# A gated mix of linear attention and a feed-forward layer: where early low parts are stored, where the key-value bursts stand, and where the fold of wq is done

## The chip, the cores and the metric

The kernel runs on one core of one Trainium2 chip. The metric is the device time of one execution in microseconds (us): the kernel before took 517.11 us in the median of three runs. The engines are named as the profile names them: PE is TensorE (PEld its weight loads), DVE is VectorE, ACT is ScalarE, POOL is GpSimd, and SP is SyncE, which here only issues transfers (DMAs).

## The reference

The input `x` has 2048 rows of 512. The output is `g * a + (1 - g) * b`, where the gate `g` is a sigmoid of one dot product per row.

```
a: qkv = x @ wqkv;  pq, pk = q, k times w_phi per head (32 heads of 16)
   phi = concat(softmax(p), softmax(-p))          for q and for k
   kv  = sum over rows of phi_k (x) v;  z = sum of phi_k
   o   = (phi_q kv) / (phi_q z + 1e-6);  a = o @ wo
b: h = relu(x @ w1 + b1) ** 2  (512 -> 1792);  b = h @ w2 + b2
out = g * a + (1 - g) * b
```

All of it is float32.

## The kernel before

**Products in three parts.** Every large operand is split into a high part (rounded to the type `fp32r`) and a low part (the remainder). ACT casts the high part, DVE subtracts to get the low part (`split`, L65 and L68). `mm3` (L73 to L75) then makes three matmuls: high by high, low by high, high by low. A tile of 128x512 has 256 KB.

**Two sweeps over the rows.** The 1792 hidden units are 14 chunks of 128, 7 to a sweep. Each sweep goes over four blocks of 512 rows. A work item `t` is one chunk in one block: `up` makes the hidden chunk `u` (12 matmuls, then relu and square on ACT and a split), and `down` adds it to the block's four output tiles `d0` to `d3` (12 matmuls). `up` runs two items ahead of `down` (`LAG`). In the first sweep the keys and values are made beside this work, in the second the queries and the attention's output.

**FFN weights.** The first sweep uses chunks 0 to 6 in each of its four blocks. In block 0 each weight is fetched (`fetch`) into one of four staging tiles `in` and split (`ready_later`). Its low part is also stored in DRAM by `keep` (tile `lkept`). In blocks 1 to 3, `again` fetches the weight and loads the stored low part, and `again_ready` only casts the high part on ACT. The high and low tiles of w1 and of w2 come from rings of three buffers (`fpool`, `NSTR`), so the fourth tile must wait until the first was used, and, where it is stored, until its store has landed. The very first product of w1 chunk 0 is done in plain float32 and needs no low part.

**Keys and values.** For each of eight pairs `p` of row tiles, seven products (`p1` to `p7`) make k (already multiplied by w_phi) and v, by a scheme that saves one of eight block products. Three accumulators take turns in two PSUM banks: `kx` and `kz` share one bank, `ky` has the other. `features` reads `kx` four times on DVE (maximum, minimum and two subtractions, L347 to L350), ACT takes the exponential, and DVE sums, inverts and multiplies (L355, L357, L361). So `kz` can't begin before those four reads are done. `do_kv` is the key-value burst: 64 products of 32x32 into one PSUM tile `kvps` of the ring that `u` uses.

**The fold.** `fold("q")` multiplies wq by w_phi: 64 small matmuls (`foldq`) that fill both buffers of the `u` ring and both PSUM banks of the keys and values. Four DVE transposes (L222, `wqin`) empty these.

**What sets the order.** `at(slot, f, ...)` puts a step into a table that the main loop reads, two slots to a work item. A scheduling layer below the kernel then places each instruction in its engine's queue by its own estimate of when operands are ready. `tc.high_priority` moves instructions ahead, and `tc.issue_after` forces one behind another. Each engine runs its queue strictly in order, so an instruction that waits holds all behind it. SP's queue is one of these: at most eight transfers are under way, since each waits for the landing of the eighth before it.

Of the kernel before, what the change touches and what calls it, by code (L numbers as in the profile page):

```python
# [18 lines left out]
NK = D // P  # L19
SB = 512  # L20
NB = S // SB
NC = SB // P
NF = F // P
NFH = NF // 2
LAG = 2
# [3 lines left out]
NPAIR = S // P // 2  # L29
NSTR = 3  # L30
AHEAD = 150
SUMS = ("t1", "t2", "t15", "k2")


@with_exitstack
def tile_gated_mix(ctx: ExitStack, tc: tile.TileContext, xT, xn, wqT, wkT, wphi, wv, wo, w1, b1, w2, b2, gw, out):
    nc = tc.nc
# [14 lines left out]
    st, up_w, down_w = {}, {}, {}  # L52
# [47 lines left out]
    raw = {}  # L100
# [29 lines left out]
    def ready_later(nm, fc, *elo):  # L130
        with tc.issue_after(st["act"].ins):
            ready(nm, fc, *elo)
# [67 lines left out]
    def fold(nm):  # L200
        wph, t = st["wphi"], st["wT", nm]
        pss = [ps_u.tile([P, 512], F32, tag="u", name=f"fold{nm}{r}") for r in range(2)]
        pss += [p.tile([P, 512], F32, tag="s", name=f"fold{nm}") for p in banks]

        def mm(g, r, q):
            rows, cols = slice(32 * r, 32 * r + 32), slice(g * P + 32 * r, g * P + 32 * r + 32)
            return nc.tensor.matmul(pss[r][32 * q:32 * q + 32, g * P:(g + 1) * P], wph[rows, cols],
                                    t[g][rows, :].rearrange("r (k q i) -> r k q i", q=4, i=32)[:, :, q, :],
                                    start=True, stop=True, skip_group_check=True)


        todo = [(g, r, q) for g in range(NK) for q in range(4) for r in range(4)]
        with ExitStack() as stack:
            for i, x in enumerate(todo):
                st["up"] = mm(*x)
                if i < 4:
                    stack.enter_context(tc.issue_after(st["up"].ins))
        w = work.tile([P, 2, 4, NG, 32], F32, tag="phiT", name=f"w{nm}in", bufs=1).rearrange(
            "p u r g s -> p (u r g s)").rearrange("p (k g r s) -> p k g r s", k=NK, g=NK, r=4)
        for r in range(4):  # L220
            with tc.high_priority(offset=AHEAD):
                nc.vector.transpose(w[:, :, :, r, :].rearrange("p k g s -> p g k s"),  # L222
                                    pss[r].rearrange("p (g k i) -> p g k i", g=NK, i=32))
        st["w", nm] = [w[:, k].rearrange("p g r s -> p (g r s)") for k in range(NK)]

    def foldq_load():
# [105 lines left out]
    def project(c, xs, ws, nm):  # L332
        ps = bank(nm)
        sc = slice(c * P, (c + 1) * P)
        for k in range(NK):
            mm3(ps, xs[k], ws[k], sc, ALL, k == 0, k == NK - 1)
        return ps

    def exps(ps, tag="e"):

        pv = ps.rearrange("p (h f) -> p h f", f=DH)
        mx = small.tile([P, H], F32, tag="mx", name="mx")
        mn = small.tile([P, H], F32, tag="mn", name="mn")
        e = work.tile([P, H, 2, DH], F32, tag=tag, name="e", bufs=2 if tag == "e" else 1)
        bc = lambda t: t.unsqueeze(2).to_broadcast([P, H, DH])
        with tc.high_priority(offset=AHEAD):
            nc.vector.tensor_reduce(mx, pv, AX.X, ALU.max)  # L347
            nc.vector.tensor_reduce(mn, pv, AX.X, ALU.min)
            nc.vector.tensor_tensor(e[:, :, 0, :], pv, bc(mx), ALU.subtract)
            nc.vector.tensor_tensor(e[:, :, 1, :], bc(mn), pv, ALU.subtract)  # L350
        ef = e.rearrange("p h t f -> p (h t f)")
        nc.scalar.activation(ef, ef, AF.Exp)  # L352
        e3 = e.rearrange("p h t f -> p (h t) f")
        sm = small.tile([P, 2 * H], F32, tag="sm", name="sm")
        nc.vector.tensor_reduce(sm, e3, AX.X, ALU.add)  # L355
        r = small.tile([P, 2 * H], F32, tag="r", name="r")
        nc.vector.reciprocal(r, sm)  # L357
        return e3, r
# [114 lines left out]
    def down(t, c, dps):  # L473
        sw, b, i = work_list[t]
        end = i == NFH - 1 or t == last - 2 and c == NC - 1
        st["down"] = mm3(dps[c], hid[t], down_w[sw * NFH + i], slice(c * P, (c + 1) * P), ALL, i == 0, end)
# [13 lines left out]
    def start():  # L490
        w = work.tile([P, 2, 4, NG, 32], F32, tag="phiT", name="win", bufs=1).rearrange("p u r g s -> p (u r g s)")
        t = st["xr", 0] = [work.tile([P, 2 * D], F32, tag="tb", name="xin", bufs=2) for _ in range(2)]
        raw["w1", 0] = w[:, :D]
        xs = [t[k // 2][:, k % 2 * D:(k % 2 + 1) * D] for k in range(NK)]
        for k in range(NK):
            nc.sync.dma_start(xs[k], xT[0, :, k, :])
        nc.scalar.dma_start(w[:, :D], w1[0])
        fetch("w1", 1, w[:, D:2 * D])
        fetch("w1", 2, w[:, 2 * D:3 * D])
        fetch("w2", 0, w[:, 3 * D:])  # L500
        fetch("w1", 3)
        fetch("w2", 1)
        t = [wpool.tile([P, 512], F32, tag=tag, name="fold") for tag in ("T40h", "T30h", "T30l", "T31h", "T31l")]
        st["wphi"] = t[0]
        nc.sync.dma_start(t[0], wphi)
        load_fold("k", wkT, t[1:])
        fetch("w1", 4)
        fetch("w2", 2)
        ps = ps_u.tile([P, SB], F32, tag="u", name="u")
        st["x", 0] = []  # L510
        for k in range(NK):
            kk = slice(k * P, (k + 1) * P)
            with tc.issue_after(st["up"].ins):
                st["up"] = nc.tensor.matmul(ps, raw["w1", 0][:, kk], xs[k], start=k == 0, stop=k == NK - 1)
            hi, lo = x_tiles(0, k)
            split(xs[k], hi, lo, nc.scalar, nc.vector)
            st["x", 0].append((hi, lo))

        t = raw.pop(("w1", 1))
        hi, lo = up_w[1] = ffn_tiles("w1", 1)  # L520
        for j in (slice(0, P), slice(P, 512)):
            nc.scalar.activation(hi[:, j], t[:, j], AF.Copy)
        nc.vector.tensor_tensor(lo, t, hi.bitcast(F32), ALU.subtract)
        i = ready("w1", 2)
        with tc.issue_after(i.ins):
            hid[0] = hidden(0, ps)
        ready_later("w2", 0)
        with tc.issue_after(st["up"].ins):
            do_up(1)
        ready_later("w1", 0)  # L530
        fetch_v()

    def do_x(b):
# [10 lines left out]
            mm3(ps, x, st["W", op, kk], slice(0, P), ALL, first and kk == 0, last and kk == 1, skip_group_check=True)  # L544

    def features(n, ps):
        e3, r = exps(ps, "ez" if n % 3 == 2 else "e")
        st["phi", n] = scaled(e3, r, nc.vector)

    def kept(tag):  # L550
# [2 lines left out]
    def total(o, ps, t):  # L553
        with tc.high_priority(offset=AHEAD):
            nc.vector.tensor_tensor(o, ps, t, ALU.add)
# [47 lines left out]
            nc.vector.tensor_tensor(kvs, kvs, ps, ALU.add)  # L603

    def do_q(b, n, c):
        st["q", n] = exps(project(c, st["x", b], st["wa"], "q"))

    def do_q_scaled(n, c):
        phi = q_phi(n, *st.pop(("q", n)))
# [40 lines left out]
    SL = 2 * NFH  # L650
    steps = {}

    def at(slot, f, *a):
        steps.setdefault(int(slot), []).append(lambda: f(*a))
# [6 lines left out]
        at(2 * fc - 1, ready_later, "w2", fc)  # L661
    for nm, fc, s in (("w1", 5, 2), ("w2", 3, 2), ("w1", 6, 4), ("w2", 4, 4), ("w2", 5, 6), ("w2", 6, 8)):
        at(s, fetch, nm, fc)
    for fc in range(NFH):
        at(max(2 * (fc - LAG), 1) + 1, keep, "w1", fc)
        at(2 * fc + 1, keep, "w2", fc)
    for t in range(NFH, NB * NFH):
        at(2 * t - 8, again, "w1", t % NFH)
        at(2 * t - 6, again_ready, "w1", t % NFH)
        at(2 * t - 4, again, "w2", t % NFH)  # L670
        at(2 * t - 2, again_ready, "w2", t % NFH)

    for kk in range(2):
        for op, s in (("B11", 4), ("B22", 5), ("T2", 6), ("B21", 6), ("T1", 7), ("T3", 8), ("T4", 9)):
# [5 lines left out]
        at(made, rows_make, p)  # L680
        at(split_at, rows_ready, p)
    at(16, foldq_load)
    at(19, fold, "q")
    at(20, foldq_move)
    for p, s in enumerate((8, 13.5, 20, 25.2, 30.4, 35.6, 40.8, 46)):
        for f, d in ((p1, 0), (p6, 1), (p2, 1), (p5, 3), (p7, 3), (p3, 4), (p4, 5)):
            at(s + d, f, p)
        at(min(s + 8, NB * SL - 2), do_kv, p)
    for b in range(NB):
        for c in range(NC):  # L690
            s = b * SL + 2 * c if b else 7 + c
# [21 lines left out]
    for p in range(NB * NC // 2):  # L713
        n, s = 2 * p, 54 + 6 * p + 2 * (p > 0)
        q, late = divmod(n, NC)[0], p == NB * NC // 2 - 1
        t = s + 12 - late + 2 * (p == 0)
# [17 lines left out]

    warm_up()
    start()
    dps = None
    for t, (sw, b, i) in enumerate(work_list):
        for f in steps.get(2 * t, ()):
            f()  # L740


        with tc.issue_after(st["down"].ins) if 0 < t <= LAG else nullcontext():
# [3 lines left out]
        if i == 0:  # L747
            dps = [ps_d.tile([P, 512], F32, tag="d", name=f"d{c}") for c in range(NC)]


        now = () if t == last - 1 else (t - 1, t) if t == last else (t,)

        with tc.issue_after(st["up"].ins) if t < LAG else nullcontext():
            for c in range(NC):
                if t == last and c == NC - 1:
                    break
                for u in now:
                    down(u, c, dps)
        if t == 1:
            with tc.issue_after(st["down"].ins):  # L760
                do_up(t + LAG)
# [8 lines left out]
        for c in range(NC):  # L770
            n = b * NC + c
# [69 lines left out]
```

## Time and profile before

| | |
|---|---|
| runs of the kernel before | 516.75, 517.11, 517.11 us |
| the profiled execution | 515.52 us, its span 513.8 us |
| PE, DVE, ACT, POOL busy | 98%, 79%, 50%, 14% of the span |
| granted clock | 1.0 throughout |

The profiled execution has 1.72 us outside of its span. It is 1.59 us below the median of the other runs. A matmul of 128x512 is shown some 390 ns long, but the next one starts 0.23 us later: matmuls overlap, so a busy PE can still be a PE that does less than it could. The distance from start to start is the better measure of a lost moment.

### The profile page before, as it was taken

To read this page: it belongs to the slowest core of one execution; us is meant where nothing else is said; L and a number is where in the kernel's file an instruction comes from. 1 tells how busy PE (TensorE), PEld (TensorE's weight loads), DVE (VectorE), ACT (ScalarE), POOL (GpSimd) and SP (SyncE) were. 2 spreads that over 40 slices of the span, in tenths; PEclk is the share of its full clock that TensorE was granted. 3 is DMA by queue.
4 is the path that set the end of the run, shared out by engine and by line. 5 is a ranking of instruction groups with operands and counts; after the bars stand their busy time and mean duration, and the time that the engine had idled before them with its cause. 6 is when DMAs were issued, how large, how long until landed. Compare 5 with 4: busy or idle time off the path is not lost.

```text
span 513.8 us, 9521 instructions
## 1 busy us (share of the span) xinstructions
PE 503.5 (98%) x3616; PEld 404.0 (79%) x3616; DVE 404.1 (79%) x640; ACT 254.6 (50%) x434; POOL 73.6 (14%) x77
## 2 busy tenths in 40 slices
PE   9899989799999999999999999999999999999997
PEld 4678868588888888788888878788787878788876
DVE  4879897875969786969689988988779677797724
ACT  6589572464537527355574545242625353333530
POOL 5303020200231000000004040301111111201100
PEclk9999999999999999999999999999999999999999
DMA  8998889683475775664648343213143321032102
GB/s 295 325 348 320 281 288 315 202 298 102 162 248 150 251 236 184 226 205 122 220 143 296 114 139 105 96 44 101 34 147 125 84 78 47 4 100 83 40 23 82
DMA packets 52869, 85.58 MB, mean 167 GB/s; under 512 B 8152, under 2 KB 14552, under 8 KB 52824
## 3 DMA queue, kind: packets, MB, share of 16 engines
q1 hardware_dynamic: 52504, 84.58, 50.7%
q8 instruction: 28, 0.46, 0.4%
q10 hardware_dynamic: 288, 0.39, 0.2%
q14 instruction: 17, 0.14, 0.1%
q0 software_dynamic: 32, 0.01, 0.0%
HBM read 57.15 MB, written 21.50 MB: 153 GB/s over the span
## 4 chain that ended last, share of the span: by engine, by line
PE 82%; DVE 7%; DMA 5%; ACT 4%; issue 1%; SPq 1%; DVEq 0%; ACTq 0%
PE u L73 8%; PE d L73 8%; PE d L74 8%; PE d L75 8%; PE u L75 8%; PE u L74 8%; PE q L73 3%; PE q L75 3%; PE q L74 3%; PE att L73 3%; PE att L75 3%; PE att L74 3%; PE kvps L370 2%; PE num L416 2%; PE ky L73 2%; PE ky L74 2%
## 5 line engine op out<-in xcount | busy, mean ns | idle before, releaser
L451 ACT ACTIVATE r<-u,b1c 128x512 f32<-128x512 f32 x56 | 38.3, 685 | 148.9 <-PE u L75 148.8
L379 POOL TENSOR_TENSOR ez<-e,z 128x512 f32<-128x512 f32 x32 | 41.7, 1325 | 279.5 <-ACT e L352 160.4
L73 PE MATMUL d<-w2h,hh 128*128 128x512 f32 x160 | 62.8, 393 | 0.2 <-DVE row L786 0.2
L73 PE MATMUL u<-xh,w1h 128*128 128x512 f32 x152 | 59.9, 394 | 2.5 <-DVE wqin L222 2.3
L74 PE MATMUL d<-w2l,hh 128*128 128x512 f32 x160 | 62.3, 389 | 0.0
L75 PE MATMUL d<-w2h,hl 128*128 128x512 f32 x160 | 62.3, 389 | 0.0
L75 PE MATMUL u<-xh,w1l 128*128 128x512 f32 x152 | 59.3, 390 | 1.4 <-DVE w1l L68 1.4
L74 PE MATMUL u<-xl,w1h 128*128 128x512 f32 x152 | 59.2, 389 | 0.0
L355 DVE TENSOR_REDUCE sm<-e 128x64 f32<-128x1024 f32 x32 | 39.0, 1217 | 20.2 <-ACT e L352 20.2
L68 DVE TENSOR_TENSOR hl<-r,hh 128x512 fp32r<-128x512 f32 x56 | 38.6, 689 | 18.3 <-ACT hh L65 18.3
L403 ACT ACTIVATE phiT<-tb 32x256 f32<-32x256 f32 x64 | 26.5, 413 | 32.1 <-DVE tb L397 31.4
L352 ACT ACTIVATE e<-e 128x1024 f32<-128x1024 f32 x32 | 33.8, 1056 | 17.2 <-DVE e L350 16.9
L73 PEld LDWEIGHTS u<-xh,w1h 128*128 128x128 f32 x152 | 28.5, 188 | 10.5 <-DVE wqin L222 2.8
L65 ACT ACTIVATE hh<-r 128x512 fp32r<-128x512 f32 x56 | 35.3, 631 | 1.6
L73 PEld LDWEIGHTS d<-w2h,hh 128*128 128x128 f32 x160 | 30.0, 188 | 7.5 <-DVE row L786 0.7
L452 ACT ACTIVATE r<-r 128x512 f32<-128x512 f32 x56 | 35.2, 628 | 1.3
L75 PEld LDWEIGHTS d<-w2h,hl 128*128 128x128 f32 x160 | 30.0, 188 | 6.3
L74 PEld LDWEIGHTS d<-w2l,hh 128*128 128x128 f32 x160 | 30.0, 188 | 6.0
L75 PEld LDWEIGHTS u<-xh,w1l 128*128 128x128 f32 x152 | 28.5, 188 | 7.8 <-DVE w1l L68 1.9
L270 POOL TENSOR_TENSOR row<-xin 128x256 f32<-128x256 f32 x16 | 16.0, 1006 | 123.5 <-DVE S4ol L68 32.7
L74 PEld LDWEIGHTS u<-xl,w1h 128*128 128x128 f32 x152 | 28.5, 188 | 5.7
L381 DVE TENSOR_REDUCE dz<-ez 128x64 f32<-128x1024 f32 x16 | 19.4, 1211 | 9.4 <-POOL ez L379 9.3
(544 smaller groups left out, 1162.7 us busy)
## 6 DMA issues: line engine op xcount, KB each, us to landing
in<-in_w SPq DMA_DIRECT2D x66, 256.0 KB, 3.1
phiT<-tb SPq DMA_DIRECT2D x192, 32.0 KB, 1.9
w1l<-lkept SPq DMA_DIRECT2D x21, 256.0 KB, 3.5
w2l<-lkept SPq DMA_DIRECT2D x21, 256.0 KB, 3.4
xin<-in_xT SPq DMA_DIRECT2D x16, 256.0 KB, 5.7
xkept<-xh SPq DMA_DIRECT2D x16, 256.0 KB, 4.5
xkept<-xl SPq DMA_DIRECT2D x16, 256.0 KB, 3.9
in<-in_xn SPq DMA_DIRECT2D x16, 256.0 KB, 3.7
```

The costliest lines, as they stand in the source:

```text
L65: i = nc.scalar.activation(hi, src, AF.Copy)
L68: st["low"] = elo.tensor_tensor(lo, src, hi.bitcast(F32), ALU.subtract)
L73: nc.tensor.matmul(o, ah[:, sa], bh[:, sb], start=first, stop=False, **kw)
L74: nc.tensor.matmul(o, ah[:, sa], bl[:, sb], start=False, stop=False, **kw)
L75: return nc.tensor.matmul(o, al[:, sa], bh[:, sb], start=False, stop=last, **kw)
L352: nc.scalar.activation(ef, ef, AF.Exp)
L355: nc.vector.tensor_reduce(sm, e3, AX.X, ALU.add)
L379: nc.gpsimd.tensor_tensor(ez[:, hs, :], e3[:, hs, :], zbc[half], ALU.mult)
L381: nc.vector.tensor_reduce(dz, ez, AX.X, ALU.add)
L403: nc.scalar.activation(dst, src, AF.Copy)
L451: nc.scalar.activation(r, ps, AF.Relu, bias=b1c[:, fc:fc + 1])
L452: nc.scalar.activation(r, r, AF.Square)
```

## The change

It has four parts.

1. `KEPT_LATE` names three low parts, of w1 chunks 0 and 1 and of w2 chunk 0. They are no longer stored in block 0, and that of w1 chunk 0 is not made there at all. In block 1 these three weights are fetched and split as in block 0, and then stored for blocks 2 and 3.
2. The burst of pair `p - 1` stands behind product `p5` of pair `p` in the table, and ahead of `p7`; before it had a slot of its own, eight slots behind the start of its pair.
3. `fold("q")` stands in the middle of the down group of work item 9, behind `d1`, with `issue_after` on both sides, and what follows it is forced behind its transposes (`st["turn"]`).
4. `features` and `do_q` are cut in two (`exps`, `sums`), and for row tile 3 the second half (`normed`) is put behind the fold.

```
+FOLD_AT = 9, 3
+KEPT_LATE = ("w1", 0), ("w1", 1), ("w2", 0)
...
     def features(n, ps):
-        e3, r = exps(ps, "ez" if n % 3 == 2 else "e")
+        st["e", n] = exps(ps, "ez" if n % 3 == 2 else "e")
+        if n != FOLD_AT[1]:
+            normed(n)
+
+    def normed(n):
+        e3, r = sums(st.pop(("e", n)))
         st["phi", n] = scaled(e3, r, nc.vector)
...
-    for fc in range(NFH):
-        at(max(2 * (fc - LAG), 1) + 1, keep, "w1", fc)
-        at(2 * fc + 1, keep, "w2", fc)
-    for t in range(NFH, NB * NFH):
-        at(2 * t - 8, again, "w1", t % NFH)
-        at(2 * t - 6, again_ready, "w1", t % NFH)
-        at(2 * t - 4, again, "w2", t % NFH)
-        at(2 * t - 2, again_ready, "w2", t % NFH)
+    for t in range(NB * NFH):
+        for nm, s in (("w1", 2 * t - 8), ("w2", 2 * t - 4)):
+            late = (nm, t % NFH) in KEPT_LATE
+            if t >= NFH:
+                first = late and t < 2 * NFH
+                at(s, fetch if first else again, nm, t % NFH)
+                at(s + 2, ready_later if first else again_ready, nm, t % NFH)
+            if t // NFH == late:
+                at(max(s + 5, 2), keep, nm, t % NFH)
...
-    at(19, fold, "q")
+    at(20, normed, FOLD_AT[1])
     at(20, foldq_move)
-        at(min(s + 8, NB * SL - 2), do_kv, p)
+        if p:
+            todo.append((do_kv, s + 3 + (p == 1), p - 1))
+        todo += [(p7, s + 3 + (p == 1), p), (p3, s + 4, p), (p4, s + 5, p)]
...
+        with tc.issue_after(st["turn"].ins) if t == FOLD_AT[0] + 1 else nullcontext():
...
+                if t == FOLD_AT[0] and c == NC // 2:
+                    with tc.issue_after(st["down"].ins):
+                        fold("q")
+                with tc.issue_after(st["up"].ins) if t == FOLD_AT[0] and c >= NC // 2 else nullcontext():
+                    for u in now:
+                        down(u, c, dps)
```

What this makes of the engines' queues is seen at three places. (Line numbers are 2 to 20 higher in the changed kernel. A number behind an underscore only tells buffers apart; `w1l3` is the low part of w1 chunk 3, `S0`, `T10` and so on are operands of the keys and values.)

DVE at the start of the program, before:

```order
L68 TENSOR_TENSOR w1l0_224<-win_133,w1h0_223 128x512
L68 TENSOR_TENSOR hl_254<-r_250,hh_253 128x512
L68 TENSOR_TENSOR w2l1_258<-in_146,w2h1_257 128x512
L68 TENSOR_TENSOR w2l2_370<-in_160,w2h2_369 128x512
L68 TENSOR_TENSOR S0ol0_377<-row_286,S0oh0_375 128x512
L68 TENSOR_TENSOR S0ol1_378<-row_287,S0oh1_376 128x512
L222 STREAM_TRANSPOSE wkin_360<-foldk0_292 128x4x4x32
L222 STREAM_TRANSPOSE wkin_360<-foldk1_293 128x4x4x32
L222 STREAM_TRANSPOSE wkin_360<-foldk_294 128x4x4x32
L222 STREAM_TRANSPOSE wkin_360<-foldk_295 128x4x4x32
L68 TENSOR_TENSOR w1l3_234<-in_144,w1h3_233 128x512
L68 TENSOR_TENSOR w1l4_366<-in_158,w1h4_365 128x512
```

The same place of DVE now:

```order
L70 TENSOR_TENSOR w1l3_230<-in_144,w1h3_229 128x512
L70 TENSOR_TENSOR hl_250<-r_246,hh_249 128x512
L70 TENSOR_TENSOR w2l1_254<-in_146,w2h1_253 128x512
L70 TENSOR_TENSOR w1l4_359<-in_158,w1h4_358 128x512
L70 TENSOR_TENSOR w2l2_363<-in_160,w2h2_362 128x512
L70 TENSOR_TENSOR S0ol0_370<-row_279,S0oh0_368 128x512
```

The low part of w1 chunk 0 is gone from here, that of chunk 3 stands in its place, and both it and chunk 4's stand ahead of the transposes.

PE at the first key-value burst, in block 1, before:

```order
L75 MATMUL d3_967<-w2h0_700,hl_729 128x512
L370 MATMUL kvps_1002<-e_671,vext0_114 32x32 x32
L73 MATMUL kz_1068<-T10h_554,S1_737 128x512
L74 MATMUL kz_1068<-T10l_555,S1_737 128x512
L75 MATMUL kz_1068<-T10h_554,S1_737 128x512
L73 MATMUL kz_1068<-T11h_558,S1_737 128x512
L74 MATMUL kz_1068<-T11l_559,S1_737 128x512
L75 MATMUL kz_1068<-T11h_558,S1_737 128x512
L73 MATMUL ky_898<-T30h_592,S1_737 128x512
L74 MATMUL ky_898<-T30l_593,S1_737 128x512
L370 MATMUL kvps_1002<-e_834,vext1_115 32x32 x32
```

PE at the same burst now (the six matmuls of `kz` stand ahead of these rows, between the fifth and the sixth matmul of `u_1013`):

```order
L77 MATMUL u_1013<-xh1_3_605,w1l3_781 128x512
L374 MATMUL kvps_1033<-e_661,vext0_114 32x32 x2
L75 MATMUL d0_960<-w2h0_768,hh_718 128x512
L76 MATMUL d0_960<-w2l0_769,hh_718 128x512
L77 MATMUL d0_960<-w2h0_768,hl_719 128x512
L374 MATMUL kvps_1033<-e_661,vext0_114 32x32 x2
L75 MATMUL d1_961<-w2h0_768,hh_718 128x512
L76 MATMUL d1_961<-w2l0_769,hh_718 128x512
L77 MATMUL d1_961<-w2h0_768,hl_719 128x512
L374 MATMUL kvps_1033<-e_661,vext0_114 32x32
L75 MATMUL d2_962<-w2h0_768,hh_718 128x512
```

The `up` of chunk 3 and `kz` moved ahead of the down group, and the burst, in two pieces before, is now in five: two, two, one and one of its products stand between the `d` tiles, and 58 behind `d3`. The other bursts moved behind the six matmuls of `kz`; that of pair 5, in two pieces before, is now whole.

DVE around the transposes of the fold, before:

```order
L350 TENSOR_TENSOR e_1157<-mn_1156,k2_1153 128x32x16
L355 TENSOR_REDUCE sm_1163<-e_1157 128x64
L68 TENSOR_TENSOR hl_1188<-r_1184,hh_1187 128x512
L357 RECIPROCAL r_1165<-sm_1163 128x64
L318 SCALAR_TENSOR_TENSOR in_1169,lg_1084<-in_1169,gwb_100 128x512
L361 TENSOR_TENSOR e_1157<-e_1157,r_1165 128x1024
L222 STREAM_TRANSPOSE wqin_1259<-foldq0_1191 128x4x4x32
L222 STREAM_TRANSPOSE wqin_1259<-foldq1_1192 128x4x4x32
L222 STREAM_TRANSPOSE wqin_1259<-foldq_1194 128x4x4x32
L222 STREAM_TRANSPOSE wqin_1259<-foldq_1193 128x4x4x32
```

The same place of DVE now:

```order
L352 TENSOR_TENSOR e_1153<-mn_1152,k2_1149 128x32x16
L70 TENSOR_TENSOR hl_1179<-r_1175,hh_1178 128x512
L224 STREAM_TRANSPOSE wqin_1256<-foldq0_1188 128x4x4x32
L224 STREAM_TRANSPOSE wqin_1256<-foldq1_1189 128x4x4x32
L224 STREAM_TRANSPOSE wqin_1256<-foldq_1190 128x4x4x32
L224 STREAM_TRANSPOSE wqin_1256<-foldq_1191 128x4x4x32
L359 TENSOR_REDUCE sm_1279<-e_1153 128x64
```

The sum, the reciprocal, the gate's dot product (L318) and the multiplication (L361) moved from ahead of the transposes to behind them, and the bank of `kx` (`foldq_1193` before, `foldq_1190` now) is emptied third instead of fourth.

More of the change, by code (lines that the diff above doesn't have):

```diff
@@ L221, in fold @@
             with tc.high_priority(offset=AHEAD):
-                nc.vector.transpose(w[:, :, :, r, :].rearrange("p k g s -> p g k s"),
-                                    pss[r].rearrange("p (g k i) -> p g k i", g=NK, i=32))
+                st["turn"] = nc.vector.transpose(w[:, :, :, r, :].rearrange("p k g s -> p g k s"),
+                                                 pss[r].rearrange("p (g k i) -> p g k i", g=NK, i=32))
         st["w", nm] = [w[:, k].rearrange("p g r s -> p (g r s)") for k in range(NK)]
@@ L352, in exps, with sums @@
         nc.scalar.activation(ef, ef, AF.Exp)
-        e3 = e.rearrange("p h t f -> p (h t) f")
+        return e.rearrange("p h t f -> p (h t) f")
+    def sums(e3):
         sm = small.tile([P, 2 * H], F32, tag="sm", name="sm")
@@ L529, in start @@
             do_up(1)
-        ready_later("w1", 0)
+        raw.pop(("w1", 0))
         fetch_v()
@@ L605, in do_q @@
     def do_q(b, n, c):
-        st["q", n] = exps(project(c, st["x", b], st["wa"], "q"))
+        st["q", n] = sums(exps(project(c, st["x", b], st["wa"], "q")))
     def do_q_scaled(n, c):
@@ L682, in tile_gated_mix @@
     at(16, foldq_load)
-    at(19, fold, "q")
+    at(20, normed, FOLD_AT[1])
     at(20, foldq_move)
-    for p, s in enumerate((8, 13.5, 20, 25.2, 30.4, 35.6, 40.8, 46)):
-        for f, d in ((p1, 0), (p6, 1), (p2, 1), (p5, 3), (p7, 3), (p3, 4), (p4, 5)):
-            at(s + d, f, p)
-        at(min(s + 8, NB * SL - 2), do_kv, p)
+    starts = (8, 13.5, 20, 25.2, 30.4, 35.6, 40.8, 46)
+    for p, s in enumerate(starts):
+        todo = [(p1, s, p), (p6, s + 1, p), (p2, s + 1, p), (p5, s + 3, p)]
+        if p:
+            todo.append((do_kv, s + 3 + (p == 1), p - 1))
+        todo += [(p7, s + 3 + (p == 1), p), (p3, s + 4, p), (p4, s + 5, p)]
+        for f, slot, q in todo:
+            at(slot, f, q)
+    at(NB * SL - 2, do_kv, NPAIR - 1)
     for b in range(NB):
@@ L738, in tile_gated_mix @@
     for t, (sw, b, i) in enumerate(work_list):
-        for f in steps.get(2 * t, ()):
-            f()
+        with tc.issue_after(st["turn"].ins) if t == FOLD_AT[0] + 1 else nullcontext():
+            for f in steps.get(2 * t, ()):
+                f()
         with tc.issue_after(st["down"].ins) if 0 < t <= LAG else nullcontext():
@@ L756, in tile_gated_mix @@
                     break
-                for u in now:
-                    down(u, c, dps)
+                if t == FOLD_AT[0] and c == NC // 2:
[4 more added lines that the diff above has]
+                        down(u, c, dps)
         if t == 1:
```

## The prediction

> **What bounds the kernel now.** I read the head of the page, then busy time by stretches, then the list of what PE waited for, and last the timeline around each wait. First the span, and four stretches (each row: length, then busy time of the engines, clock, DMA share):
>
> ```profile
> span 513.8 us, 9521 instructions
> ...
> 22.00:38.00 16.00, 14.43 (x63) 11.29 (x61) 12.77 (x22) 10.31 (x19) 0.00 (x0) 1.00 0.97 354
> 38.00:62.00 24.00, 24.00 (x107) 19.70 (x106) 23.67 (x40) 17.04 (x31) 5.06 (x4) 1.00 0.91 305
> 62.00:104.00 42.00, 37.58 (x451) 28.87 (x451) 32.16 (x55) 20.25 (x34) 6.22 (x8) 1.00 0.83 272
> 104.00:262.00 158.00, 158.00 (x1515) 130.01 (x1505) 124.53 (x204) 85.40 (x141) 9.70 (x12) 1.00 0.61 196
> ```
>
> PE (first busy figure) is the bound. It never idles from 104 to 262, where six of the seven moved bursts lie, so nothing but small change can be won there. It idles 1.57 us between 22 and 38 and 4.42 us between 62 and 104. DVE (third) is busy 23.67 of 24 us from 38 to 62: the added work lands there. Two of PE's waits there, in their list:
>
> ```profile
> PE u L73 <- DVE wqin L222: 2.3, 1, 2.3
> PE u L75 <- DVE w1l L68: 1.4, 1, 1.4
> ```
>
> **The start.** Columns of a timeline: start, duration, line; in brackets idle time and who ended it.
>
> ```profile
> 22.24 0.39 PE L74 MATMUL u<-xl,w1h 128*128 128x512 f32 x1
> 22.46 0.39 PE L73 MATMUL u<-xh,w1h 128*128 128x512 f32 x1
> 24.29 0.50 PE L75 MATMUL u<-xh,w1l 128*128 128x512 f32 x1 [1.44 <-DVE w1l L68]
> 24.62 0.40 PE L73 MATMUL u<-xh,w1h 128*128 128x512 f32 x1
> ...
> 23.54 1.32 DVE L68 TENSOR_TENSOR w1l<-in,w1h 128x512 fp32r<-128x512 f32 x2 [0.52 <-DMA lkept<-w1l]
> ```
>
> The pace is 0.23 from start to start (22.24 to 22.46). PE loses 24.29 - 22.46 - 0.23 = 1.60 waiting for the low part of w1 chunk 3. DVE made it only at 23.54, since a stored low part still held its ring buffer. The matmul behind a wait takes 0.33 instead of 0.23, so 0.10 more: 1.70 in all. In the changed order this subtraction stands in the place of w1 chunk 0's, ahead of the transposes and needing no store. I count 1.70 as gained; a smaller gain would need a new wait right behind, and there ACT's chain starts from the end of the same `u` and moves along. Six transfers of 256 KB (three stores, three loads) leave the stretch before 62, whose DMA is nearly full (0.97), and two of the stores come back within it, so transfers get earlier rather than later. The cast that is saved on ACT I count at nothing: PE is busy beside it.
>
> **Block 1.** PE, then DVE:
>
> ```profile
> 70.31 0.39 PE L75 MATMUL u<-xh,w1l 128*128 128x512 f32 x1
> 70.95 0.50 PE L73 MATMUL d<-w2h,hh 128*128 128x512 f32 x1 [0.25 <-DVE row L786]
> ...
> 73.93 0.76 PE L370 MATMUL kvps<-e,vext 128*32 128x32 f32 x64
> 76.00 0.48 PE L73 MATMUL kz<-T10h,S 128*128 128x512 f32 x1 [1.31 <-DVE e L350]
> ...
> 78.14 0.75 PE L370 MATMUL kvps<-e,vext 128*32 128x32 f32 x64
> 78.82 0.50 PE L75 MATMUL ky<-T30h,S 128*128 128x512 f32 x1
> ...
> 63.88 0.69 DVE L318 SCALAR_TENSOR_TENSOR in<-in,gwb 128x512 f32<-128x512 f32 x1 [1.97 <-DMA in<-in_xn]
> ...
> 70.15 2.72 DVE L786 SCALAR_TENSOR_TENSOR row<-d,rest,row 128x512 f32<-128x512 f32 x4
> ...
> 73.38 0.68 DVE L347 TENSOR_REDUCE mx<-kx 128x32 f32<-128x512 f32 x1
> ```
>
> The first `d` of block 1 waits 70.95 - 70.31 - 0.23 = 0.41 for DVE's row, plus 0.10 behind it: 0.51. The first half of the burst takes 2.07 until `kz` starts (73.93 to 76.00), the second 0.68 (78.14 to 78.82): `kz` waits 1.39 for the four reads of `kx`.
>
> Now `kz` stands ahead of the down group and of the burst, but behind five matmuls of the next `u`. PE reaches it at 73.93 + 0.68 less 1.70 (start), 0.41, and 3.66 of work now behind it (70.95 to 74.61), plus 5 x 0.23: about 70.0. DVE started the reads at 73.38. In the new order 2.7 of row work and one split of 0.6 stand behind them; the 1.97 of idle ahead of L318 is filled, since the reads of `k2` and one low part now stand ahead of that instruction; the start gives 1.7; three low subtractions come in ahead at 0.66 each (23.54, two in 1.32). So 73.38 - 2.7 - 0.6 - 1.97 - 1.7 + 2.0 = 68.4, and the four reads end 2.4 later, at 70.8; with the small gaps of DVE that close as well (some 1.2), at 69.6. `kz` waits between nothing and 0.8: I take 0.4. The row instructions, which follow the reads, free `d0` to `d3` 0.66 apart, while PE now needs 0.9 for each `d`: no wait.
>
> **What a piece of a burst costs.** Pair 5's burst was cut by `kz`:
>
> ```profile
> 211.80 0.40 PE L73 MATMUL kz<-T11h,S6oh 128*128 128x512 f32 x1
> 212.12 0.76 PE L370 MATMUL kvps<-e,vext 128*32 128x32 f32 x64
> 212.82 0.50 PE L74 MATMUL kz<-T11l,S6oh 128*128 128x512 f32 x1
> 213.15 0.40 PE L75 MATMUL kz<-T11h,S6ol 128*128 128x512 f32 x1
> ```
>
> Going in costs 0.09 (0.32 instead of 0.23), coming out 0.10, so 0.19 at least. The two-product piece of the fold below cost 0.52. The burst's own shape is nearer to the first: I take 0.30. The first burst goes from two pieces to five, +0.90 (0.6 to 1.6); pair 5's from two to one, -0.30. The other bursts only change places with `kz`, whose bank was free 1.4 us or more ahead of time: nothing.
>
> **The fold.** PE, ACT, DVE:
>
> ```profile
> 90.50 0.39 PE L75 MATMUL u<-xh,w1l 128*128 128x512 f32 x1
> ...
> 91.48 0.40 PE L74 MATMUL d<-w2l,hh 128*128 128x512 f32 x1
> ...
> 92.04 1.89 PE L207 MATMUL foldq<-row,in 32*32 32x128 f32 x126
> 93.86 0.50 PE L73 MATMUL d<-w2h,hh 128*128 128x512 f32 x1
> ...
> 95.80 0.39 PE L75 MATMUL d<-w2h,hl 128*128 128x512 f32 x1
> 98.52 0.50 PE L73 MATMUL u<-xh,w1h 128*128 128x512 f32 x1 [2.33 <-DVE wqin L222]
> ...
> 99.56 0.39 PE L74 MATMUL u<-xl,w1h 128*128 128x512 f32 x1
> 100.40 0.47 PE L73 MATMUL kx<-B110h,xh 128*128 128x512 f32 x1 [0.46 <-DVE wqin L222]
> ...
> 90.92 0.69 ACT L451 ACTIVATE r<-u,b1c 128x512 f32<-128x512 f32 x1 [5.10 <-PE u L75]
> 92.31 1.06 ACT L352 ACTIVATE e<-e 128x1024 f32<-128x1024 f32 x1 [0.70 <-DVE e L350]
> ...
> 93.92 0.63 ACT L65 ACTIVATE hh<-r 128x512 fp32r<-128x512 f32 x1
> ...
> 88.46 0.69 DVE L318 SCALAR_TENSOR_TENSOR in<-in,gwb 128x512 f32<-128x512 f32 x1 [2.95 <-DMA in<-in_xn]
> ...
> 97.76 2.50 DVE L222 STREAM_TRANSPOSE wqin<-foldq 128x512 f32<-128x512 f32 x4
> ```
>
> The early piece goes: 91.48 - 90.50 holds two large matmuls, 0.98 - 0.46 = 0.52. Behind the fold PE loses 98.52 - 95.80 - 0.23 = 2.49 and 100.40 - 99.56 - 0.23 = 0.61, plus 0.10 and 0.08 behind them: 3.28.
>
> New, counted from the end of the last `u` before: PE does `d0`, `d1` (1.36), the fold (1.82 and 0.1), `d2`, `d3` (1.36 and 0.1) and wants the `u` buffer at 4.75, the bank of `kx` four matmuls later, at 5.65. Ahead of the transposes DVE now has just `hl`, which waits for ACT: from 90.92 to 94.55 ACT takes 3.63, of which 0.70 was idle, waiting for `e`. So hl is ready at 0.2 + 2.93 + 0.7 = 3.8 and the transposes (0.62 each) end at 4.5 for `u` and 5.7 for `kx`: a wait of 0.1. With the 0.70 kept, 0.8. I take 0.1, as DVE was late there through the 2.95 it waited for a transfer, which the smaller load makes earlier.
>
> **The sum**, against the profiled execution: 1.70 + 0.51 + 1.39 + 0.52 + 3.28 + 0.30 - 0.90 - 0.4 - 0.1 = 6.3. So 515.52 - 6.3 = 509.2. The median of the runs is 1.59 higher; the same saving from 517.11 gives 510.8.
>
> **The rivals.**
> A. DVE comes late in block 1, because the fill I assume doesn't happen (a transfer lands late, the three low parts cost more). Then `kz` waits 1.39 as before and `d` 0.51: 1.5 more than I took, 512.3. For it: 23.67 of 24 busy. Against: 1.97 of idle that the order can fill.
> B. One low part meets GpSimd. This row is the neighbour of its four instructions (5.06 busy from 38 to 62):
>
> ```profile
> 47.51 1.06 DVE L68 TENSOR_TENSOR T31l<-wvin,T31h 128x512 fp32r<-128x512 f32 x1
> ```
>
> A subtraction takes 1.06 there instead of 0.66. One low part of the three stands beside them: 0.4 on DVE, `kz` later by as much, 511.2. [...]
> C. The wait behind the fold stays, since `hl` or the fold's operands come late: 2.5 of the 3.28 remain, 513.3. Against: the order has four instructions fewer ahead of the transposes.
> D. Slower. ACT's queue holds the casts of w2 chunk 0 and w1 chunk 3 between its relus, and the first of these transfers is issued only when w1 chunk 1's new subtraction has freed the staging tile. ACT's longest such wait in the profile is
>
> ```profile
> ACT w2h L121 <- DMA in<-in_w: 5.6, 1, 5.6
> ```
>
> Two of these in a row stop PE at the `u` of chunk 3 for 11.2 less some 0.7 of slack: 10.5 against 6.3, so 521.3. It decides when they add up to over 7. Against: fewer transfers are in flight than before.
> E. It doesn't do what it says, each freed wait being replaced by the next one late: 517.
>
> **The numbers.** Forecast 0.57, A 0.13, B 0.08, C 0.08, D 0.08, E 0.03, and 0.03 for more than I count (the gain of 6.8 without the new waits, and small gaps: 509.8). What this kernel's measurement tells from no change is some 0.2%, 1.0 us. So faster 0.89, same 0.03, slower 0.08. The range reaches from 509.6 to 513.6: it holds the forecast, A, B and C and leaves out D and E.
>
> **What would show it.** The list of PE's waits no longer has `w1l` at the start, `kz` behind `e`, or `u` behind `wqin` beyond some tenths; five pieces of the first burst cost 0.3 each; DVE's transposes start right behind `hl`; PE is without idle time from 104 less 6 on. I am wrong if PE idles at the `u` of chunk 3 in block 1 (ACT behind a transfer), at `kz`, or at `foldq` itself for its operands.

## The result, and the profile after

The changed kernel took 509.01 us (median of four runs, 508.79 to 509.30), beside 517.11 us for the kernel before on the same chip. The ratio is 0.9843, its 95% interval 0.9826 to 0.9860. The forecast was 510.8 with a range from 509.6 to 513.6: right in sign and kind, 1.8 us short, and 0.6 us outside of the range.

The profiled execution took 508.94 us. The head of its page, and the same stretches as before (length, then busy time of PE, its weight loads, DVE, ACT, POOL, the granted clock, DMA share):

```profile
span 507.2 us, 9515 instructions
...
22.00:38.00 16.00, 15.87 (x71) 12.80 (x70) 13.35 (x23) 12.18 (x22) 0.00 (x0) 1.00 0.99 343
38.00:62.00 24.00, 24.00 (x107) 19.79 (x106) 24.00 (x42) 16.51 (x30) 5.07 (x4) 1.00 0.84 281
62.00:104.00 42.00, 41.99 (x418) 32.55 (x417) 35.05 (x61) 21.13 (x35) 7.50 (x8) 1.00 0.84 277
```

PE's idle time is gone: 0.13 us from 22 to 38 (before 1.57) and 0.01 from 62 to 104 (before 4.42). DVE is now busy for all of the stretch from 38 to 62. The list of PE's waits has one entry left, of the `warm` matmuls at the program's start:

```profile
PE warm L491 <- PEq L850: 0.8, 1, 0.8
```

Between the profiled executions the saving is 515.52 - 508.94 = 6.58 us, where the prediction's sum was 6.3. Between the medians it is 8.1. So the terms are nearly right, and what is missing is the step from the one to the other. On another chip, where both kernels ran later, the medians were 516.17 and 509.30 us, 6.9 apart.

Two stretches of PE of the changed kernel, and below them ACT and DVE where they mattered. Block 1:

```profile
68.61 0.39 PE L77 MATMUL u<-xh,w1l 128*128 128x512 f32 x1
...
69.74 0.39 PE L76 MATMUL u<-xl,w1h 128*128 128x512 f32 x1
70.05 0.47 PE L75 MATMUL kz<-T10h,S 128*128 128x512 f32 x1
...
72.89 0.39 PE L77 MATMUL u<-xh,w1l 128*128 128x512 f32 x1
73.20 0.26 PE L374 MATMUL kvps<-e,vext 128*32 128x32 f32 x4
73.39 0.50 PE L75 MATMUL d<-w2h,hh 128*128 128x512 f32 x1
73.73 0.39 PE L76 MATMUL d<-w2l,hh 128*128 128x512 f32 x1
...
77.50 1.20 PE L374 MATMUL kvps<-e,vext 128*32 128x32 f32 x116
78.63 0.50 PE L75 MATMUL ky<-T30h,S 128*128 128x512 f32 x1
...
65.46 0.63 ACT L123 ACTIVATE w2h<-in 128x512 fp32r<-128x512 f32 x1 [1.13 <-DMA in<-in_w]
67.28 0.63 ACT L123 ACTIVATE w1h<-in 128x512 fp32r<-128x512 f32 x1 [1.09 <-DMA in<-in_w]
```

The last matmul of the `u` of chunk 2 starts at 68.61; before, the same one started at 70.31. `kz` comes 0.31 behind its predecessor in place of 0.23, so it lost 0.08. The pieces of the burst are plain to see: two products (four records) of 0.26 us, and a `d` behind each.

The fold:

```profile
88.04 0.39 PE L77 MATMUL u<-xh,w1l 128*128 128x512 f32 x1
...
89.72 1.91 PE L209 MATMUL foldq<-row,in 32*32 32x128 f32 x128
91.55 0.50 PE L75 MATMUL d<-w2h,hh 128*128 128x512 f32 x1
...
92.81 0.40 PE L77 MATMUL d<-w2h,hl 128*128 128x512 f32 x1
93.12 0.50 PE L75 MATMUL u<-xh,w1h 128*128 128x512 f32 x1
...
93.92 0.39 PE L75 MATMUL u<-xh,w1h 128*128 128x512 f32 x1
94.31 0.50 PE L75 MATMUL kx<-B110h,xh 128*128 128x512 f32 x1
...
91.75 0.69 DVE L70 TENSOR_TENSOR hl<-r,hh 128x512 fp32r<-128x512 f32 x1 [2.31 <-ACT hh L67]
92.36 2.50 DVE L224 STREAM_TRANSPOSE wqin<-foldq 128x512 f32<-128x512 f32 x4
```

DVE waits for ACT, then does `hl` and goes straight on to the transposes, as forecast. PE takes the buffer of `u` at 93.12, 0.08 late, and the bank of `kx` at 94.31, 0.16 late.

### The profile page after: what moved, and what is told of

The parts are those of the page before. It is cut to its first block, busy times and chain, and to the rows that moved or that the text cites. A ratio compares the mean times of both kernels' runs of the same rounds, so it can differ in the third digit from the quotient of the medians.

```text
span 507.2 us, 9515 instructions
## 1 busy us (share of the span) xinstructions
PE 503.0 (99%) x3616; PEld 403.9 (80%) x3616; DVE 404.0 (80%) x642; ACT 254.2 (50%) x433; POOL 75.0 (15%) x77
## 4 chain that ended last, share of the span: by engine, by line
PE 98%; ACT 1%; DVE 0%; issue 0%
PE d L75 10%; PE u L75 10%; PE d L77 10%; PE d L76 10%; PE u L76 10%; PE u L77 9%; PE q L75 3%; PE q L76 3%; PE q L77 3%; PE att L76 3%; PE att L77 3%; PE att L75 3%; PE ky L75 2%; PE ky L77 2%; PE ky L76 2%; PE kvps L374 2%
## 5 line engine op out<-in xcount | busy, mean ns | idle before, releaser
L272 POOL TENSOR_TENSOR row<-xin 128x256 f32<-128x256 f32 x16 | 17.8, 1120 | 117.4 <-DVE S4ol L70 27.6
```

## Where the other 1.5 us came from: the clock behind the fold

The prediction took the 1.59 us by which the kernel before's runs were above its profiled execution as something that both kernels have. To see what it is, the kernel before was profiled again, the changed parts were undone one at a time, and part 1 and parts 3 and 4 were each tried alone.

**The kernel before, unchanged (before_again).**

> The kernel before, once more, to see whether its profiled execution of 515.52 us was an ordinary one. In its profile the start lost 1.70 us (1.60 waiting for the low part of w1 chunk 3, which waited for a store). First theory: the other executions, at 517.1, lose 1.6 us more at a wait that the change takes away, most likely this one, since it ends with the landing of a store. Then a profile at about 517.1 (span 515.4) shows PE waiting some 3.0 us for w1l where it showed 1.4, and the rest as before. Second theory: the profiled execution was faster by a little everywhere, or outside of PE's waits. Then the waits are 1.4, 2.3 and 1.3 as before, and the span differs elsewhere.

Ten executions took 514.19 to 517.92 us, median 515.75. The profiled one, 515.71, is about as long as the first profile, but it is made up otherwise: PE comes to the wait behind the fold 0.88 us earlier (its last matmul ahead of it starts at 94.92, before at 95.80), and loses that again behind it. Stretches around this wait, first of the profile that the prediction had, then of this one (the clock is the figure behind POOL's):

```profile
94.00:98.00 4.00, 2.19 (x9) 1.47 (x9) 4.00 (x7) 2.63 (x5) 2.14 (x3) 1.00 0.41 137
98.00:102.00 4.00, 3.02 (x12) 2.24 (x13) 3.43 (x6) 0.00 (x0) 0.00 (x0) 1.00 1.00 302
```

```profile
94.00:98.00 4.00, 1.70 (x8) 1.10 (x7) 4.00 (x7) 1.42 (x3) 1.23 (x2) 1.00 0.69 202
98.00:102.00 4.00, 3.55 (x11) 2.57 (x10) 2.52 (x5) 0.00 (x0) 0.00 (x0) 0.64 1.03 373
102.00:106.00 4.00, 4.00 (x139) 3.15 (x139) 0.00 (x0) 2.35 (x4) 0.00 (x0) 0.93 0.59 194
...
99.00:99.20 0.20, 0.04 (x1) 0.00 (x0) 0.20 (x1) 0.00 (x0) 0.00 (x0) 0.88 0.96 297
102.40:102.60 0.20, 0.20 (x2) 0.12 (x1) 0.00 (x0) 0.18 (x1) 0.00 (x0) 0.59 1.06 410
```

After the wait the granted clock falls, to 0.64 and 0.93 in the mean of two of these stretches. The short ones say more exactly when: with a clock of 0.50 in between (the mean of the stretch from 98 to 102 in kept_only, below), means of 0.88 and 0.59 put its fall at 99.15 and its return at 102.56, 3.41 us later. In PE's timeline of this run:

```profile
97.60 0.50 PE L73 MATMUL u<-xh,w1h 128*128 128x512 f32 x1 [2.30 <-DVE wqin L222]
97.94 0.40 PE L74 MATMUL u<-xl,w1h 128*128 128x512 f32 x1
...
99.49 0.76 PE L73 MATMUL kx<-B110h,xh 128*128 128x512 f32 x1 [0.45 <-DVE wqin L222]
100.05 0.63 PE L74 MATMUL kx<-B110l,xh 128*128 128x512 f32 x1
100.47 0.63 PE L75 MATMUL kx<-B110h,xl 128*128 128x512 f32 x1
...
102.18 0.58 PE L75 MATMUL u<-xh,w1l 128*128 128x512 f32 x1
102.60 0.40 PE L73 MATMUL u<-xh,w1h 128*128 128x512 f32 x1
```

From 99.49 to 102.60 a matmul takes 0.43 from start to start (the first one 0.56) in place of 0.23. Seven matmuls take 3.11 us in place of 1.59: 1.5 us lost, about the offset that the prediction carried over. So the first theory's place was wrong: the start isn't longer here (that wait was 1.2). A loss of about this size lies behind the fold, and the runs below ask whether the wait there causes it and whether the change takes it away.

PE stood idle for 2.30 us up to 97.60, then worked, and the clock fell 0.11 us into the next wait (0.45, from 99.04 on). In the first profile the same two waits, of 2.33 and 0.46 us, left it at 1.00. So their length alone doesn't say whether it falls, and what sets the 3.41 us isn't shown either.

The clock doesn't fall in every execution. Of 65 executions of the kernel before on three chips, 16 had a mean clock of 0.999 or more (median 514.7 us) and 49 a lower one (median 516.5). The first profiled execution was of the rarer kind. Where the clock fell is known only of profiled executions. The clock isn't all of the spread either: those 16 reach from 513.5 to 517.2 us, which was not followed up. The executions of the other kernels are counted in the same way below.

**Parts undone and parts alone.** The low parts alone (kept_only, part 1 on the kernel before):

```
+KEPT_LATE = ("w1", 0), ("w1", 1), ("w2", 0)
...
-        ready_later("w1", 0)
+        raw.pop(("w1", 0))
...
+            if t // NFH == late:
+                at(max(s + 5, 2), keep, nm, t % NFH)
```

> The kernel before with part 1 alone (the three early low parts). First theory (the other executions wait longer at the start): 1.70 + 1.6 = 3.3 us less than 517.1, so 513.8; PE's wait for w1l is gone, and the waits for e (1.3), row and wqin stay. Second theory: 1.7 less, 515.4.

514.95 us, beside 516.37 for the kernel before on that chip (ratio 0.9973, 0.9951 to 0.9996): a gain of 1.4 us, 0.2 to 2.5 by the interval, which holds the 1.7 of the second theory and not the 3.3 of the first. In the profile the wait at the start is gone, and those for `e` and `row` with it, which the first theory had left standing. The one behind the fold has grown, and the clock dropped in 9 of 10 executions. PE's wait there, and DVE:

```profile
PE u L74 <- DVE wqin L223: 4.5, 1, 4.5
```

```profile
97.11 0.69 DVE L319 SCALAR_TENSOR_TENSOR in<-in,gwb 128x512 f32<-128x512 f32 x1 [1.82 <-DMA in<-in_xn]
97.72 0.08 DVE L319 DVE_READ_ACCUMULATOR in<-in,gwb 128x1 f32 x1
97.72 2.50 DVE L223 STREAM_TRANSPOSE wqin<-foldq 128x512 f32<-128x512 f32 x4
```

The transposes start at 97.72; in the kernel before at 97.76. DVE's gate instruction stands ahead of them and waits for a transfer, so in this execution all that PE gained ahead of this point it waits here. It took 516.59 us and was the slowest of the ten; the median's 1.4 says that more of the gain stays in most of the others. The clock fell at 96.96 here, while PE still stood idle, and came back at 103.78 (worked out as above).

The fold back at its old place (fold_undone, parts 3 and 4 undone, with the forced orders around it):

```
-    at(20, normed, FOLD_AT[1])
+    at(19, fold, "q")
...
-        if n != FOLD_AT[1]:
-            normed(n)
+        normed(n)
...
-                    with tc.issue_after(st["down"].ins):
-                        fold("q")
```

> The changed kernel with the fold of wq back at its old place and without the deferred half of features for row tile 3 (parts 3 and 4 undone). By the terms of the prediction the fold gains 3.28 + 0.52 - 0.1 = 3.7, so 509.0 + 3.7 = 512.7. First theory: just that. Second theory, in the form that the longer wait of the other executions is the one behind the fold: 5.3 more, 514.3.

514.27 us (0.9965, 0.9945 to 0.9985): 5.3 more than the changed kernel, as the second theory had it. PE waits 3.4 us behind the fold, and the clock dropped in 8 of 10 executions (median 514.3; the other two 512.2 and 512.5, near the first theory's 512.7). In the profile it fell at 98.06, 0.96 us behind the end of the wait, for 3.41 us.

The new fold alone (fold_only, parts 1 and 2 undone in the changed kernel):

> The kernel before with the fold's new place and the deferred half alone (parts 3 and 4). By the terms of the prediction 3.7 us less. First theory (the wait behind the fold also costs the clock, some 2 us in most executions): 516.4 - 3.7 - 2.0 = 510.7, with a clock of 1.0 in every execution. Second theory (the drop has another cause): 512.7, and the clock below 1.0 in most executions.

513.22 us (0.9938, 0.9917 to 0.9959). The clock was 0.999 or more in all four executions, so the drop goes with the fold's old place; whether the wait causes it is tried below, with matmuls that fill it. The time lies above both theories: in this order PE still waits 0.7 behind the fold, and the burst of pair 1 is cut by a product. So parts 3 and 4 gain some 3 us alone and some 5 beside the other two (the changed kernel's own medians on two chips lie 0.3 apart): in that company the wait that they take away is 3.4 us long and not 2.3.

The bursts back in their old slots (burst_undone, part 2 undone):

```
-            todo.append((do_kv, s + 3 + (p == 1), p - 1))
+        at(min(s + 8, NB * SL - 2), do_kv, p)
```

> The changed kernel with the key-value bursts back in their old slots (part 2 undone). By the terms of the prediction part 2 gains 0.51 + 1.39 + 0.30 - 0.90 - 0.4 = 0.9, so 509.9. In this order the first burst is again cut (a piece behind the up of chunk 2, then five pieces around the down group), so kz again stands behind a burst and waits for e. If the pieces cost 0.3 each and kz waits 1.4, it is 510 to 511. If the moved bursts gain nothing, 509.0.

511.09 us (0.9909, 0.9874 to 0.9943): part 2 is worth some 2 in the medians, not 0.9, though this order isn't the old one. The first burst is in six pieces here, two others (of pairs 1 and 5) in two, `kz` waits 0.4 (in block 1 no longer, but at pair 2) and `u` 0.7 behind the fold.

The low parts back in block 0 (kept_undone, part 1 undone):

```
-KEPT_LATE = ("w1", 0), ("w1", 1), ("w2", 0)
+KEPT_LATE = ()
...
-        raw.pop(("w1", 0))
+        ready_later("w1", 0)
```

> The changed kernel with all low parts made and stored in block 0 again (part 1 undone). In this order the first burst is whole, and kz stands behind two matmuls of u. By the terms of the prediction the start loses 1.70 again, and the four extra pieces of the burst (0.3 each, 1.2) go: 509.0 + 1.7 - 1.2 = 509.5. If DVE then frees kz and the rows late, as in the kernel before, up to 1.9 more, 511.4. The clock stays at 1.0, as the wait behind the fold is gone.

511.11 us (0.9903, 0.9882 to 0.9925), near the second of the two figures, and the clock stayed at 0.999 or more in all four. The wait at `kz` is back, and at the start PE waits again, now for the transposes of the fold of wk (`wkin`) and not for `w1l`, though the first burst is whole.

```profile
PE kz L75 <- DVE e L352: 1.5, 1, 1.5
PE u L75 <- DVE wkin L224: 1.2, 1, 1.2
```

**Is it the standing idle, or the fold's small matmuls?** Here the wait behind the fold was filled with useless matmuls (wait_filled, on the order with the fold at its old place):

```
+    def fill(ps):
+        one = nc.const_aps.tensor(1.0, (P, 512), mybir.dt.bfloat16)
+        for _ in range(NFILL):
+            with tc.issue_after(st["down"].ins):
+                st["down"] = nc.tensor.matmul(ps, zero, one, start=False, stop=False, skip_group_check=True)
...
+                if t == 9 and c == NC - 1:
+                    fill(dps[c])
```

> Fold at its old place, as in fold_undone, with 14 useless matmuls of 128x512 (zeros as one operand, added to the last output tile of work item 9) in the wait behind the fold. In that order kx stands ahead of u and has to wait for the last of the four transposes, some 0.6 us longer. First theory: PE's clock drops because PE stands idle behind the fold, for some 3.4 us after it. Then with 3.0 us of the wait filled the clock stays at 1.0 in every execution, no matmul behind the wait takes 0.43 from start to start, and the time is 512.4 (the two executions of fold_undone at full clock) + 0.6 = 513.0, although PE does more. Second theory: the drop has another cause (the small matmuls of the fold, or the run of the chip). Then most executions again show a mean clock of 0.997 or less, and the time is 514.3 + 0.6 = 514.9.

A miss for the first theory as written: 516.53 us, and the clock dropped in 8 of 10 executions. In the profiled one, which kept its clock, PE still stood idle for 1.65 us:

```profile
93.39 3.22 PE L620 MATMUL d<-const-bfloat16-1.0,zero 128*128 128x512 bf16 x14
98.26 0.47 PE L76 MATMUL kx<-B110h,xh 128*128 128x512 f32 x1 [1.65 <-DVE wqin L227]
```

So either so much idle time is enough in the other executions, or matmuls of zeros don't hold the clock, or the small matmuls ahead are the cause. Two more fills, of nearly the whole wait: one with real data (filled_real, its matmul below) and one with zeros (filled_zeros, the fill above, 22 long):

```
+                st["down"] = nc.tensor.matmul(ps, neg if i % 2 else w, hid[9][0], start=False, stop=False, skip_group_check=True)
```

> As wait_filled, with 20 matmuls of real data in the wait (a weight tile and its negative in turn, so that the sum is unchanged): 4.5 us of work in a wait of 5.0, so some 0.5 us idle. If standing idle drops the clock: 1.0 in every execution, 514.0. If the fold's own small matmuls drop it: below 1.0 in most executions, as in wait_filled, 516.4.

> As filled_real, with 22 matmuls of zeros (4.7 us). If the gate counts a matmul whatever its data: as filled_real. If it counts what the array does, zeros count as idle: below 1.0 in most executions, 516.4, while filled_real stays at 1.0.

With real data 514.71 us, and a clock of 0.999 or more in all four executions. With zeros 514.79 (513.30 to 517.81), and a drop in one of ten. ("The gate" in the second expectation is whatever sets PE's granted clock; that it counts anything was the author's guess, and no run shows it.) The fold's small matmuls are the same in all three, so they alone aren't the cause; nor do zeros drop the clock (1 of 10). Of the three that leaves the standing idle: in one and the same order of PE, 14 matmuls of zeros in the wait give 516.53 us and a drop in 8 of 10, and 22 give 514.79 and a drop in 1 of 10, so PE does more and is done 1.7 us earlier (the kernel before took 516.22 and 516.17 beside them). How much idle time drops the clock stays open. In the profile with 14 a wait of 1.65 us kept the clock, in the first profile one of 2.33 kept it, and in that of filled_zeros it was kept through this:

```profile
PE kx L76 <- DVE wqin L227: 2.7, 1, 2.7
```

Only the profiled executions show the length of the wait.

## What a piece of a burst costs, and a faster version

Five pieces of the first burst remained in the changed kernel. The first attempt (burst_whole) put the whole burst a work item later:

```
-            todo.append((do_kv, s + 3 + (p == 1), p - 1))
-        todo += [(p7, s + 3 + (p == 1), p), (p3, s + 4, p), (p4, s + 5, p)]
+            todo.append((first_kv, 18, 0) if p == 1 else (do_kv, s + 3, p - 1))
+        todo += [(p7, s + 3 + 1.5 * (p == 1), p), (p3, s + 4 + (p == 1), p), (p4, s + 5, p)]
...
+    def first_kv(p):
+        with tc.issue_after(st["down"].ins):
+            do_kv(p)
```

> The changed kernel with the first burst forced whole behind a down group, so one piece in place of five. By the price in the prediction (0.30 a piece) it gains 4 x 0.30 = 1.2 us on 509.0, so 507.8. By the profile of the changed kernel a piece of two products costs 0.51 - 0.23 + 0.11 = 0.39 less 0.04 of its own work, so 0.35: 507.6. If pieces cost only what goes in and comes out (0.19), 508.2. If the later burst makes DVE or a PSUM bank late, no gain: 509.0.

509.62 us (508.21 to 512.37): the rival. The burst is whole, but `ky` and what follows it come later, and PE waits at the fold.

```profile
PE u L75 <- DVE wqin L224: 1.6, 1, 1.6
PE warm L491 <- PEq L854: 0.8, 1, 0.8
PE foldq L209 <- DMA row<-in_wqT: 0.7, 1, 0.7
```

With waits such as these around the fold the clock dropped in two of six executions; the profiled one kept it.

The second attempt (burst_next, beside the changed kernel once more, after_again) keeps the burst in its slot and only forces it behind the first down group. DVE, ACT and SP then have the order of the changed kernel, and PE too but for the burst and one matmul of `ky` that moves ahead of the down group:

```
-            todo.append((do_kv, s + 3 + (p == 1), p - 1))
+            todo.append((first_kv if p == 1 else do_kv, s + 3 + (p == 1), p - 1))
```

> The changed kernel once more, on the same chip as the next three. Both theories: 509.0, and a clock of 0.999 to 1.0 in every execution.

> The changed kernel with the first burst whole and right behind the first down group of block 1, everything else in the order of the changed kernel. A piece there cost 0.35 by the changed kernel's profile, so four fewer gain 1.4: 507.6. By the 0.30 of the prediction 507.8. Rival, as in burst_whole: PE reaches the fold earlier, and the wait for its operands (0.7) and behind it (1.6) take it back: 509.0.

The changed kernel took 509.30 us on this chip (0.9855, 0.9838 to 0.9872), this one 508.30 (0.9838, 0.9823 to 0.9852): 1.0 us less, each with all four executions at full clock, and their times apart from each other (508.55 to 510.12 against 508.20 to 508.84). It is the fastest version here. PE around the burst:

```profile
76.17 0.39 PE L77 MATMUL d<-w2h,hl 128*128 128x512 f32 x1
76.49 1.30 PE L374 MATMUL kvps<-e,vext 128*32 128x32 f32 x128
77.72 0.50 PE L76 MATMUL ky<-T30l,S 128*128 128x512 f32 x1
78.06 0.40 PE L77 MATMUL ky<-T30h,S 128*128 128x512 f32 x1
```

The whole burst takes from 76.17 + 0.23 to 77.72, and 0.11 behind it: 1.43. In the changed kernel, from 72.89 to 78.63 there are thirteen large matmuls (2.95) and the burst in five pieces: 5.74 - 2.95 = 2.79, and 0.11 behind: 2.90. Four pieces more cost 1.47, or 0.37 each; the prediction had 0.30. Of this 0.09 goes in and 0.11 comes out, and 0.19 lies between the first small matmul and the next large one (73.20 to 73.39), where four records in the middle of a burst take 0.04. Of the 1.47 the medians show 1.0: in the profile of this run PE comes to `kz` 0.45 later (70.50 against 70.05), ahead of the place that was changed, and the cause of that was not followed up.

## Why the prediction came out as it did

**Start, 1.70.** Right: the last matmul of chunk 2's `u` in block 1 moved from 70.31 to 68.61, by 1.70. No new wait came up behind it. The prediction added it to the fold's term as if the two were independent; the runs show part 1 at 1.4 alone (kept_only) and some 2 beside the other parts (kept_undone).

**Block 1, 0.51 + 1.39 - 0.4 less three pieces at 0.30, so 0.60.** From there to the last `u` ahead of the fold the lead grew from 1.70 to 90.50 - 88.04 = 2.46, so 0.76. `kz` lost 0.08 and not 0.4 (DVE filled its gaps: 24.00 of 24 us busy from 38 to 62, before 23.67), `d` nothing, and the pieces cost 0.37. Two errors that partly cancel.

**Fold, 0.52 + 3.28 - 0.1 = 3.70.** `kx` starts at 94.31 behind four matmuls of `u`, before at 100.40 behind five; with 0.23 for the fifth the lead is 5.86, so the fold gave 3.40. Of the waits 0.08 and 0.16 are left, and 0.10 behind the first of them, where the prediction took 0.1.

**Pair 5, 0.30.** PE's lead is 5.98 ahead of this burst (`u` at 209.09 and 203.11) and 6.34 behind it (219.09 and 212.75): 0.36, again near the 0.37 of a piece. The last matmul of the program, before and after:

```profile
509.99 0.28 PE L75 MATMUL end<-w213h,hl 128*128 128x256 f32 x1
503.68 0.28 PE L77 MATMUL end<-w213h,hl 128*128 128x256 f32 x1
```

That PE's lead at the end is 6.31, where the sum was 6.3, is partly luck: block 1 gave 0.16 more, the fold 0.30 less, pair 5 0.06 more, and 0.09 came from places that have no term. The other 0.27 of the 6.58 lies behind PE's last matmul.

**The step that failed** is the last of the sum: "The median of the runs is 1.59 higher; the same saving from 517.11 gives 510.8." It took the offset for a constant. The later runs show that most executions of the kernel before (49 of 65) lose about 1.5 to 1.8 us to a lower clock (1.5 in the profile of before_again, 1.8 between the medians 516.5 and 514.7), that this loss lies at the very wait that the change removes or begins within 1.6 us behind it (in each of the three profiles that have it: before_again, kept_only, fold_undone), that the kernel's profiled execution was one of the fewer without, and that none of the eight executions of the changed kernel loses it. 6.3 from the terms and 1.6 from the offset give 7.9, beside 8.1 measured. On the chip where the clock of both kernels was recorded, the changed kernel is 6.1 us faster than the kernel before's three executions at full clock (515.37) and 7.1 faster than its other ten (516.4). (The clock of the first runs of the kernel before wasn't recorded; that they lost it is concluded from 65 later ones.) The clock of 1.0 in the quoted stretches was read as the clock of the kernel, but it was that of one execution.

**The rivals.** A and C didn't happen. B left no trace on PE: `kz` lost 0.08 in all. The four GpSimd instructions of that stretch took 2.93 us and three times 0.73 to 0.74; the last, beside the row shown, ran from 47.28 to 48.02, so 0.51 of it was left when the subtraction began, and the subtraction took 0.40 longer (1.06 instead of 0.66). In the changed kernel a low part of w1 ran beside the longest of them (41.01 to 43.94) from 42.66 on and took 0.68, and `T30l` from 45.66 on, beside the last (45.42 to 46.15), took 1.05. Of D, ACT did wait for the two transfers that it names, 1.13 and 1.09 us rather than 5.6, and PE didn't. E fails with the result.

## What to carry to other kernels

When the profiled execution and the median of the runs differ by more than the runs among themselves, ask which wait the difference could hang on before carrying it over: a wait that the change removes may cost more in other executions than in the one shown. Here a PE wait of some 2 us was worth more than its length: 49 of 65 executions had a lower clock, and in the profile of one of them (before_again) seven matmuls behind the wait took 3.11 us in place of 1.59. And gains ahead of a point where PE waits for another engine can be lost there in part until that point moves too (here DVE's transposes, of which the gate instruction was ahead), so the gains of such parts needn't add up one by one: parts 3 and 4 gave some 3 us alone and some 5 beside the others.

## What was not expected of the hardware

The mean granted clock was below 0.999 in 49 of 65 executions of the kernel before. Two profiles of this program, with PE idle for 2.33 and 0.46 us and for 2.30 and 0.45, differ in it: 1.00 throughout in the first, 0.50 for a time in the second. It fell with PE at work again, 0.96 us behind the end of the wait (fold_undone); 1.55 us behind the end of the long wait, within the short one (before_again); and while PE still waited (kept_only). It came back 3.41 us later in the first two and 6.82 us later in kept_only. With 14 matmuls of zeros in the wait it was kept in 2 of 10 executions, with 22 in 9 of 10, with 20 of real data in 4 of 4.
